# Feed-forward blocks that run over the batch boundary in a spectral mixing and ELU feed-forward kernel

## The chip, the cores and the metric

The kernel runs on one core of a Trainium2 chip. A core has TensorE (PE, matmuls into PSUM; its weight loads are listed apart as PEld), VectorE (DVE), ScalarE (ACT), GpSimd (POOL) and SyncE (SP, which issues most DMAs). The metric is device time in microseconds (us). The page and the trace come from one profiled execution.

## What is computed

The input x has 8 batches of 3008 tokens with 256 features. Each batch goes through a real Fourier transform along the tokens, a complex 256 x 256 product with bias, a soft threshold and the inverse transform. The result, taken as 24064 tokens, goes through a feed-forward layer of width 2048 with ELU.

```
X = np.fft.rfft(x, axis=1)
Yr = Xr @ w_r - Xi @ w_i + b_r
Yi = Xr @ w_i + Xi @ w_r + b_i
Yr = np.sign(Yr) * np.maximum(np.abs(Yr) - lam, 0.0)    # and Yi; lam = 0.01
y = np.fft.irfft(Yr + 1j * Yi, n=3008, axis=1)
h = y.reshape(24064, 256) @ w_in                        # 256 -> 2048
g = np.where(h > 0.0, h, np.exp(np.minimum(h, 0.0)) - 1.0)
out = g @ w_out                                         # 2048 -> 256
```

## The kernel before

**Feed-forward.** A batch is cut into blocks of TB = 512 tokens: five of 512 and one of 448. The hidden width is 16 tiles of 128, taken in pairs, so a block has NPAIR = 8 steps, a batch PER = 48, the program 384. Step i has two halves. `front(i)` (L675) runs four bf16 matmuls (L688), two hidden tiles by two halves of the 256 features, from yT (the transposed output of the inverse transform) into the PSUM tile hps, and then Exp on ScalarE (L701) into Et. `elu` (L719) clips Et, and one step later `finish_elu` (L706) makes gT with one VectorE operation. `back(i)` (L729) runs eight matmuls of 256 columns (L749, weights from gT, two hidden tiles by four groups of 128 tokens; in a block of 448 the last group has 64) that add into the PSUM tiles ps_o. It is issued LAG = 2 steps behind its front. After the eighth step of a block, ps_o is copied to osb (L763; L767 for the groups of a 448 block's end) and stored to DRAM by up to two DMAs for each group of 128 tokens (L774).

**Transforms.** The next batches' transforms are cut into units, of which a step takes at most one ahead of its front:

- A (L128): first stage of the transform, two matmuls from a loaded x tile, a cast by ScalarE; after each second unit a store DA (512 KB). Six units a batch, made two batches ahead of use.
- X (L165): reads Z, which `load_Z` loads back from DA; eight units of eight matmuls.
- M (L200): the complex product, four matmuls of 512 columns, twelve units; its threshold is done by VectorE and GpSimd.
- B (L227): first stage of the inverse, eight matmuls, six units; after each second unit a store DB (512 KB).
- Y (L268): reads Bs, which `load_Bs` (four DMAs of 384 KB, one for each fourth of the tokens) loads back from DB; eight matmuls of 94 columns and a cast into yT. Eight units, two for each fourth of the tokens: units 0 and 1 make tokens 0 to 751.

`plan(b)` (L783) writes the order by hand: `mid` is the list, `lead` the step at which it begins (1 in the first batch, else 0). Before, steps 0 to 3 carry Y2 to Y5, 4 to 11 the X units, 12 to 37 the M, B and A units with Y6 and Y7 among them, and the steps 38 to 44 and 46 are bare. Y0 and Y1 of the next batch stand at steps 45 and 47 (`yn`). The Bs loads follow A2 (step 34), the Z loads A5 (step 37).

**What depends on that.** The loop (L826) calls a step `free` if it has nothing planned. In a free step the clip is shared by GpSimd and VectorE (L724) and gT is made by L713; in a step with an M unit ScalarE does the whole clip (L698, L699); else VectorE clips alone (L726) and L715 makes gT. In calm free steps each third hps comes from the units' PSUM pool psF (one buffer), else from psH (two). Where a block ends in a step that is not free (`split`), the first copy of ps_o goes to VectorE. TensorE takes its instructions in the order written, and so does SP its DMA issues: stores of DA and DB, loads of Z and Bs, and outputs stand in one line and wait for each other's turn.

Of the kernel before, what the change touches and what calls it, by code (L numbers as in the profile page):

```python
# [9 lines left out]
AF = mybir.ActivationFunctionType  # L10
BF16 = mybir.dt.bfloat16
F32 = mybir.dt.float32
# [17 lines left out]
def kernel(  # L30
# [11 lines left out]
    nc = tc.nc  # L42
    P = nc.NUM_PARTITIONS

    B, S, D = x.shape
    assert D == 256 and S == N1 * N2
    DFF = moe_w_in.shape[1]
    E = moe_w_out.shape[1]
# [14 lines left out]
    w_in_s = constp.tile([P, 2, DFF], BF16, name="w_in_s")  # L63
# [24 lines left out]

    TB = 512
    NPAIR = NFT // 2  # L90
    NBLK = (S + TB - 1) // TB
    PER = NBLK * NPAIR
    LAG = 2
    n = B * PER
    WT = 2 * N1 * 8
# [10 lines left out]
    yT_of = {}  # L106
# [192 lines left out]
    with tc.tile_pool(name="stagep", bufs=1) as stagep:  # L299
# [90 lines left out]
        c1 = mix(dve, qcol, -2.0, pcol, ALU.mult, ALU.add)  # L390
        c0 = col(dve, c1, -1.0, ALU.mult, 1.0, ALU.add)
# [265 lines left out]
    for u in range(2):  # L657
# [9 lines left out]
    psO = ctx.enter_context(  # L667
        tc.tile_pool(name="psO", bufs=2, space=bass.MemoryType.PSUM, reuse_waits="tile")
    )
# [2 lines left out]
    g_of = {}  # L672
    po_of = {}

    def front(i, third, on_act):  # L675
        b, r = divmod(i, PER)
        blk, fp = divmod(r, NPAIR)
        bs = blk * TB
        nb = min(TB, S - bs)
        yT = yT_of[b]  # L680
        if third:
            hps = psF.tile([P, 2, TB], F32, name="hps", tag="fps")
        else:
            hps = psH.tile([P, 2, TB], F32, name="hps", tag="hps")
        for s in range(2):
            ft = 2 * fp + s
            for dt in range(2):
                nc.tensor.matmul(  # L688
                    hps[:, s, 0:nb], lhsT=w_in_s[:, dt, ft * P : ft * P + P],
                    rhs=yT[:, dt, bs : bs + nb], start=(dt == 0), stop=(dt == 1),  # L690
                )
        Et = late3.tile([P, 2, TB], F32, name="Et", tag="Et")
        E_ = Et[:, :, 0:nb]
        if i == n - 1:
            for s in range(2):
                nc.scalar.activation(E_[:, s], hps[:, s, 0:nb], AF.Exp)
        elif on_act:
            nc.scalar.activation(E_, hps[:, :, 0:nb], AF.Relu, scale=-1.0)  # L698
            nc.scalar.activation(E_, E_, AF.Exp, scale=-1.0)  # L699
        else:  # L700
            nc.scalar.activation(E_, hps[:, :, 0:nb], AF.Exp)  # L701
        return hps, Et, nb

    late_elu = []

    def finish_elu():  # L706
        for i, hps, Et, nb, whole in late_elu:
            E_, h_ = Et[:, :, 0:nb], hps[:, :, 0:nb]
            gT = late3.tile([P, 2, TB], F32R, name="gT", tag="gT")
            for s in range(2) if i == n - 1 else (slice(0, 2),):  # L710
                o, h, e = gT[:, s, 0:nb], h_[:, s], E_[:, s]
                if whole:
                    nc.vector.scalar_tensor_tensor(o, e, -1.0, h, ALU.add, ALU.max)  # L713
                else:
                    nc.vector.scalar_tensor_tensor(o, h, 0.0, e, ALU.max, ALU.add)  # L715
            g_of[i] = gT
        late_elu.clear()

    def elu(i, hps, Et, nb, on_pool, on_act):  # L719

        E_ = Et[:, :, 0:nb]
        if on_pool:
            for eng, s in ((nc.gpsimd, 1), (nc.vector, 0)):
                eng.tensor_scalar(E_[:, s], E_[:, s], 1.0, 0.0, ALU.min, ALU.max)  # L724
        elif not on_act:
            nc.vector.tensor_scalar(E_, E_, 1.0, -1.0, ALU.min, ALU.add)  # L726
        late_elu.append((i, hps, Et, nb, on_pool or on_act))

    def back(i, split):  # L729
        b, r = divmod(i, PER)  # L730
        blk, fp = divmod(r, NPAIR)
        bs = blk * TB
        nb = min(TB, S - bs)
        gT = g_of.pop(i)
        nsub = (nb + P - 1) // P
        if fp == 0:
            po_of[b, blk] = [
                psO.tile([P, 2, E], F32, name="ps_o", tag="outp") for _ in range((nsub + 1) // 2)
            ]
        po = po_of[b, blk]  # L740
        nq = (nsub + 1) // 2
        order = [(q, s) for q in range(nq) for s in range(2)]
        if i == n - 1:
            order = [(q, s) for s in range(2) for q in range(nq)]
        for q, s in order:
            ft = 2 * fp + s
            for i_ in range(2 * q, min(2 * q + 2, nsub)):
                t0, t1 = i_ * P, min(i_ * P + P, nb)
                nc.tensor.matmul(  # L749
                    po[q][0 : t1 - t0, i_ % 2, :], lhsT=gT[:, s, t0:t1],  # L750
                    rhs=w_out_r[:, ft, :], start=(ft == 0 and i_ % 2 == 0),
                    stop=(ft == NFT - 1), skip_group_check=True,
                )
        if fp < NPAIR - 1:
            return
        osb = late2.tile([P, 4, E], F32, name="osb", tag="osb")
        ov = out[b * S : b * S + S, :].rearrange("(r w j) e -> w r j e", w=4, j=8)
        last = i == n - 1
        for q in range(nq):
            k = min(2, nsub - 2 * q)  # L760
            copy = nc.vector.tensor_copy if (last and q) or (split and q == 0) else nc.scalar.copy
            if nb >= (2 * q + k) * P:
                copy(osb[:, 2 * q : 2 * q + k, :], po[q][:, 0:k, :])  # L763
            else:
                for e in range(k):
                    rows = min(P, nb - (2 * q + e) * P)
                    copy(osb[0:rows, 2 * q + e, :], po[q][0:rows, e, :])  # L767
            for i_ in range(2 * q, 2 * q + k):
                t, end = bs + i_ * P, min(bs + i_ * P + P, bs + nb)
                while t < end:  # L770
                    w, r0 = t // WT, t % WT // 8
                    t1 = min(end, (w + 1) * WT)
                    p0, n8 = t - bs - i_ * P, (t1 - t) // 8
                    (nc.scalar if last and i_ % 2 == 0 else nc.sync).dma_start(  # L774
                        ov[w, r0 : r0 + n8], osb[p0 : p0 + 8 * n8, i_, :]
                    )
                    t = t1
        del po_of[b, blk]

    def put(kind, b, *a):  # L780
        return ({"A": unit_A, "X": unit_X, "M": unit_M, "B": unit_B, "Y": unit_Y}[kind], (b, *a))

    def plan(b):  # L783

        f0 = [[] for _ in range(PER)]
        f1 = [[] for _ in range(PER)]
        n1, n2 = b + 1, b + 2
        mid = [("X", u) for u in range(8)] + [
# [4 lines left out]
        ]  # L793
        if n1 < B:
            lead, seq = int(b == 0), [("y", u) for u in range(2, 6)] + mid
            seq.insert(20, ("y", 6))
            seq.insert(24, ("y", 7))
            xs = (3, 8, 13)
            yn = (45, 47)
        else:  # L800
            lead, seq = 0, [("y", u) for u in range(2, 8)]
        for t, u in enumerate(seq, lead):
            if u[0] == "y":
                f0[t].append(put("Y", b, u[1]))
            elif u[0] == "A":
                if n2 < B:
                    f0[t].append(put("A", n2, u[1]))
            else:
                f0[t].append(put(u[0], n1, *u[1:]))
            if u == ("A", 2):  # L810
                f1[t] += [(load_Bs, (n1, w)) for w in range(4)]
            if u == ("A", 5) and n2 < B:
                f1[t] += [(load_Z, (n2, s0, s1)) for s0, s1 in ((0, 8), (8, NS))]
        if b == 0:
            f1[xs[0]].append((lambda: gate(Z_of[1][:, 16, 0:1]), ()))
        if n2 < B:
            for ci in range(3):
                f1[xs[ci]].append((load_x, (n2, ci)))
        if n1 < B:
            for u in range(2):  # L820
                f0[yn[u]].append(put("Y", n1, u))
        return f0, f1

    f0 = f1 = None
    bare = 0
    for i in range(n + LAG):  # L826
        if i < n:
            r = i % PER
            if r == 0:
                f0, f1 = plan(i // PER)  # L830
# [6 lines left out]
            on_act = any(f is unit_M for f, a in f0[r])  # L837
            h = front(i, calm and bare % 3 == 2, on_act)
# [42 lines left out]
```

## Time and profile before

| What | Value |
| --- | --- |
| time, median of 3 runs (lowest to highest) | 926.57 us (925.47 to 928.17) |
| profiled execution: its own time | 927.22 us |
| its span in the trace | 925.4 us |
| granted TensorE clock | 0.999 |
| busy: PE, DVE, ACT, POOL | 898.0, 754.0, 697.3, 268.3 us |
| back matmuls L749 | 3072 |
| front matmuls L688 (of 1536, as recorded) | 1463 |
| moved by DMA | 106.21 MB |

The median of the runs is what a change is measured by; the profiled execution is one run, of which everything about single instructions is known. A line of the profile's groups reads: source line, engine, operation, output <- inputs, partitions x elements, count | busy us, mean ns of one | idle time of the engine before them and what ended it. A line of the timeline reads: start in us, duration in us, engine, line, operation, count. Some matmul records are missing, weight loads are all there; so steps are timed here by the first weight load of their front (L688), of which each step has four.

### The profile page before, as it was taken

Reading aid. Unit: us, or ns where it says so; the run is one execution under the profiler, and the core shown is the slowest. Engines: PE = TensorE matmul, PEld = TensorE weight load, DVE = VectorE, ACT = ScalarE, POOL = GpSimd, SP = SyncE. Lnnn points to the kernel's source line nnn. Section 1 sums busy time; section 2 is a strip of 40 time slices with the busy share of each in tenths; the row PEclk is TensorE's granted clock in tenths of the full one; section 3 lists DMA queues with packets and bytes.
Section 4 is the critical chain, followed back from the end, with each engine's and each line's share of the span. In section 5 each row is a group of like instructions: output and inputs, shape, how many; then the busy total and the mean of one; then the engine's idle time right before and its main releaser. Section 6 shows DMA issues by size and latency. Waiting matters only on the chain.

```text
span 925.4 us, 16719 instructions
## 1 busy us (share of the span) xinstructions
PE 898.0 (97%) x6477; PEld 643.8 (70%) x6583; DVE 754.0 (81%) x898; ACT 697.3 (75%) x783; POOL 268.3 (29%) x352
## 2 busy tenths in 40 slices
PE   8879999999999999999999999999999999999997
PEld 3447667776677676776677766777777767677775
DVE  7868778887788777897788877887778877789997
ACT  6667787777868788687787778777786878676664
POOL 6801441133310441205402153113331044322332
PEclk9999999999999999999999999999999999999999
DMA  8984216621383224722166031752138002411011
GB/s 263 355 253 141 91 47 191 193 69 46 94 225 113 69 68 126 220 88 90 48 181 204 24 91 46 211 174 69 47 95 224 21 24 68 114 48 44 23 46 44
DMA packets 90655, 106.21 MB, mean 115 GB/s; under 512 B 5264, under 2 KB 81296, under 8 KB 87216
## 3 DMA queue, kind: packets, MB, share of 16 engines
q1 hardware_dynamic: 84320, 77.61, 30.0%
q0 software_dynamic: 5968, 27.26, 9.0%
q8 instruction: 51, 0.84, 0.4%
q10 hardware_dynamic: 288, 0.26, 0.1%
q14 instruction: 28, 0.23, 0.1%
HBM read 55.31 MB, written 49.81 MB: 114 GB/s over the span
## 4 chain that ended last, share of the span: by engine, by line
PE 72%; DVE 16%; ACT 3%; issue 3%; DMA 3%; POOL 1%; SPq 0%; DVEq 0%; ACTq 0%; POOLq 0%
PE ps_o L749 29%; PE hps L688 28%; PE mps L189 8%; DVE gT L713 7%; DVE Et L724 3%; PE bps L238 2%; DVE gT L715 2%; ACT Et L701 2%; PE yps L276 2%; PE aps L143 2%; DVE Et L726 2%; PE xps L174 1%; DMA Z<-DA 1%; DMA DA<-A 1%; DMA xt<-in_x_dram 1%
## 5 line engine op out<-in xcount | busy, mean ns | idle before, releaser
L749 PE MATMUL ps_o<-w_out_r,gT 128*128 128x256 f32 (+1 forms) x3072 | 486.4, 301 | 0.7 <-DVE gT L713 0.5
L749 PEld LDWEIGHTS ps_o<-w_out_r,gT 128*128 128x128 f32 (+1 forms) x3072 | 407.1, 186 | 61.2 <-DVE gT L713 14.4
L688 PE MATMUL hps<-yT,w_in_s 128*128 128x512 bf16 (+1 forms) x1463 | 383.5, 375 | 8.6 <-DVE gT L715 1.4
L701 ACT ACTIVATE Et<-hps 128x1024 f32<-128x1024 f32 (+1 forms) x299 | 300.7, 1006 | 85.7 <-PE hps L688 77.6
L713 DVE SCALAR_TENSOR_TENSOR gT<-Et,hps 128x1024 fp32r<-128x1024 f32 (+2 forms) x187 | 220.0, 1177 | 60.9 <-ACT Et L699 38.3
L715 DVE SCALAR_TENSOR_TENSOR gT<-hps,Et 128x1024 fp32r<-128x1024 f32 (+1 forms) x198 | 240.3, 1214 | 15.5
L688 PEld LDWEIGHTS <-w_in_s 128*128 128x128 bf16 x1536 | 131.5, 98 | 140.0 <-issue 21.7
L726 DVE TENSOR_SCALAR Et<-Et 128x1024 f32<-128x1024 f32 (+1 forms) x198 | 135.9, 686 | 45.5 <-ACT Et L701 40.1
L204 POOL TENSOR_SCALAR clip<-yb 128x512 f32<-128x512 f32 x84 | 51.6, 615 | 331.9 <-DVE yb L196 262.5
L724 POOL TENSOR_SCALAR Et<-Et 128x512 f32<-128x512 f32 (+1 forms) x102 | 64.8, 636 | 269.9 <-ACT Et L701 268.7
L698 ACT ACTIVATE Et<-hps 128x1024 f32<-128x1024 f32 x84 | 86.2, 1026 | 72.1 <-PE hps L688 71.0
L205 POOL TENSOR_TENSOR Y<-yb,clip 128x512 bf16<-128x512 f32 x84 | 107.3, 1277 | 7.0
L196 DVE TENSOR_TENSOR yb<-mps,bias_bc 128x512 f32<-128x512 f32 x96 | 65.8, 688 | 32.2 <-PE mps L189 23.6
L699 ACT ACTIVATE Et<-Et 128x1024 f32<-128x1024 f32 x84 | 88.8, 1057 | 2.7
L126 ACT CAST XT<-xps 128x768 bf16<-128x768 f32 x61 | 48.6, 799 | 16.6 <-PE xps L174 16.6
L126 ACT CAST yT<-yps 128x752 bf16<-128x752 f32 x63 | 49.5, 786 | 15.0 <-PE yps L276 15.0
L126 ACT CAST A<-aps 128x1024 bf16<-128x1024 f32 x45 | 45.3, 1010 | 15.7 <-PE aps L143 13.4
L189 PE MATMUL mps<-wcat_s,XT 128*128 128x512 bf16 x183 | 55.2, 379 | 1.1
L724 DVE TENSOR_SCALAR Et<-Et 128x512 f32<-128x512 f32 (+1 forms) x102 | 54.6, 536 | 0.3 <-ACT Et L701 0.2
L189 PE MATMUL mps<-wcat_r,XT 128*128 128x512 bf16 x171 | 53.5, 385 | 0.7 <-ACT XT L126 0.6
L189 PEld LDWEIGHTS <-XT 128*128 128x128 bf16 x384 | 30.3, 98 | 29.5 <-ACT XT L126 0.9
L251 ACT CAST Bz<-bps 128x1024 bf16<-128x1024 f32 x46 | 45.9, 999 | 3.2 <-PE bps L238 3.2
(104 smaller groups left out, 402.8 us busy)
## 6 DMA issues: line engine op xcount, KB each, us to landing
xt<-in_x_dram POOLq DMA_DIRECT2D x21, 1024.0 KB, 5.4
out_dram<-osb SPq DMA_DIRECT2D x158, 128.0 KB
Bs<-DB SPq DMA_DIRECT2D x32, 384.0 KB
DA<-A SPq DMA_DIRECT2D x21, 512.0 KB
DB<-Bz SPq DMA_DIRECT2D x21, 512.0 KB
Z<-DA SPq DMA_DIRECT2D x7, 1152.0 KB
Z<-DA SPq DMA_DIRECT2D x11, 384.0 KB
xt<-in_x_dram POOLq DMA_DIRECT2D x6, 512.0 KB, 6.3
```

The source lines that it names most:

```text
L126: nc.scalar.copy(dst, src)
L189: nc.tensor.matmul(ps, lhsT=XT[:, dt, c, o : o + P], rhs=wm[:, dt, :], start=(m == 0 and dt == 0), stop=(m == 1 and dt == 1),)
L205: nc.gpsimd.tensor_tensor(Y_of[b, q][:, i, :], yb[:], clip[:], ALU.subtract)
L688: nc.tensor.matmul(hps[:, s, 0:nb], lhsT=w_in_s[:, dt, ft * P : ft * P + P], rhs=yT[:, dt, bs : bs + nb], start=(dt == 0), stop=(dt == 1),)
L698: nc.scalar.activation(E_, hps[:, :, 0:nb], AF.Relu, scale=-1.0)
L699: nc.scalar.activation(E_, E_, AF.Exp, scale=-1.0)
L701: nc.scalar.activation(E_, hps[:, :, 0:nb], AF.Exp)
L713: nc.vector.scalar_tensor_tensor(o, e, -1.0, h, ALU.add, ALU.max)
L715: nc.vector.scalar_tensor_tensor(o, h, 0.0, e, ALU.max, ALU.add)
L724: eng.tensor_scalar(E_[:, s], E_[:, s], 1.0, 0.0, ALU.min, ALU.max)
L726: nc.vector.tensor_scalar(E_, E_, 1.0, -1.0, ALU.min, ALU.add)
L749: nc.tensor.matmul(po[q][0 : t1 - t0, i_ % 2, :], lhsT=gT[:, s, t0:t1], rhs=w_out_r[:, ft, :], start=(ft == 0 and i_ % 2 == 0), stop=(ft = ...
```

## The change

The feed-forward no longer sees batches: 24064 tokens are 47 blocks of 512, so the program has 376 steps, 47 for each batch's plan. A block may hold the end of one batch and the beginning of the next. In such a block (there are seven) each front matmul becomes two, one for each batch's yT, with 64 and 448, 128 and 384, 192 and 320, or 256 and 256 columns; a group of 128 tokens that holds both batches is stored by DMAs of its own for each. Every operation on hps, Et, gT and osb has full width.

Y0 and Y1 of the next batch stand at steps 38 and 39. A5 stands at step 37, in the first batch at step 40, behind them. The end of the order is B4, A0, B5, A1, Bs loads, A2 to A5; before it was A0, B4, A1, B5, A2, Bs loads, A3 to A5. B4 thus follows the last M unit, and the Bs loads are issued at step 33 (34 in the first batch, whose list begins a step later).

```diff
-    NBLK = (S + TB - 1) // TB
-    PER = NBLK * NPAIR
+    PER = S * NPAIR // TB
...
+    def pieces(t, k):
+        out_, c = [], 0
+        while c < k:
+            b, r = divmod(t + c, S)
+            e = min(k, c + S - r)
+            out_.append((b, r, c, e))
+            c = e
+        return out_
...
         for s in range(2):
             ft = 2 * fp + s
-            for dt in range(2):
-                nc.tensor.matmul(
-                    hps[:, s, 0:nb], lhsT=w_in_s[:, dt, ft * P : ft * P + P],
-                    rhs=yT[:, dt, bs : bs + nb], start=(dt == 0), stop=(dt == 1),
-                )
+            for b, t0, c0, c1 in pieces(blk * TB, TB):
+                for dt in range(2):
+                    nc.tensor.matmul(
+                        hps[:, s, c0:c1], lhsT=w_in_s[:, dt, ft * P : ft * P + P],
+                        rhs=yT_of[b][:, dt, t0 : t0 + c1 - c0],
+                        start=(dt == 0), stop=(dt == 1),
+                    )
...
-            for i_ in range(2 * q, min(2 * q + 2, nsub)):
-                t0, t1 = i_ * P, min(i_ * P + P, nb)
+            for i_ in range(2 * q, 2 * q + 2):
                 nc.tensor.matmul(
-                    po[q][0 : t1 - t0, i_ % 2, :], lhsT=gT[:, s, t0:t1],
+                    po[q][:, i_ % 2, :], lhsT=gT[:, s, i_ * P : i_ * P + P],
...
-            if nb >= (2 * q + k) * P:
-                copy(osb[:, 2 * q : 2 * q + k, :], po[q][:, 0:k, :])
-            else:
-                for e in range(k):
-                    rows = min(P, nb - (2 * q + e) * P)
-                    copy(osb[0:rows, 2 * q + e, :], po[q][0:rows, e, :])
+            copy(osb[:, 2 * q : 2 * q + 2, :], po[q][:])
...
-            ("M", 4, 1), ("B", 3), ("M", 5, 0), ("M", 5, 1), ("A", 0), ("B", 4), ("A", 1),
-            ("B", 5), ("A", 2), ("A", 3), ("A", 4), ("A", 5),
+            ("M", 4, 1), ("B", 3), ("M", 5, 0), ("M", 5, 1), ("B", 4),
+            ("A", 0), ("B", 5), ("A", 1), ("A", 2), ("A", 3), ("A", 4),
...
-            yn = (45, 47)
+            seq += [("A", 5), ("n", 0), ("n", 1)] if b else [("n", 0), ("n", 1), ("A", 5)]
...
+            elif u[0] == "n":
+                f0[t].append(put("Y", n1, u[1]))
...
-            if u == ("A", 2):
+            if u == ("A", 1):
                 f1[t] += [(load_Bs, (n1, w)) for w in range(4)]
```

More of the change, by code (lines that the diff above doesn't have):

```diff
@@ L90 @@
     NPAIR = NFT // 2
-    NBLK = (S + TB - 1) // TB
-    PER = NBLK * NPAIR
+    assert S * NPAIR % TB == 0 and S % (P // 2) == 0
+    PER = S * NPAIR // TB
     LAG = 2
@@ L673 @@
     po_of = {}
-    def front(i, third, on_act):
[L676 to L680, printed above, removed]
+    def pieces(t, k):
[6 more added lines that the diff above has]
+        return out_
+    def front(i, third, on_act):
+        blk, fp = divmod(i, NPAIR)
         if third:
@@ L686, in front @@
             ft = 2 * fp + s
-            for dt in range(2):
-                nc.tensor.matmul(
-                    hps[:, s, 0:nb], lhsT=w_in_s[:, dt, ft * P : ft * P + P],
-                    rhs=yT[:, dt, bs : bs + nb], start=(dt == 0), stop=(dt == 1),
-                )
+            for b, t0, c0, c1 in pieces(blk * TB, TB):
[5 more added lines that the diff above has]
+                    )
         Et = late3.tile([P, 2, TB], F32, name="Et", tag="Et")
-        E_ = Et[:, :, 0:nb]
+        E_ = Et[:]
         if i == n - 1:
             for s in range(2):
-                nc.scalar.activation(E_[:, s], hps[:, s, 0:nb], AF.Exp)
+                nc.scalar.activation(E_[:, s], hps[:, s], AF.Exp)
         elif on_act:
-            nc.scalar.activation(E_, hps[:, :, 0:nb], AF.Relu, scale=-1.0)
+            nc.scalar.activation(E_, hps[:], AF.Relu, scale=-1.0)
             nc.scalar.activation(E_, E_, AF.Exp, scale=-1.0)
         else:
-            nc.scalar.activation(E_, hps[:, :, 0:nb], AF.Exp)
-        return hps, Et, nb
+            nc.scalar.activation(E_, hps[:], AF.Exp)
+        return hps, Et
     late_elu = []
     def finish_elu():
-        for i, hps, Et, nb, whole in late_elu:
-            E_, h_ = Et[:, :, 0:nb], hps[:, :, 0:nb]
+        for i, hps, Et, whole in late_elu:
             gT = late3.tile([P, 2, TB], F32R, name="gT", tag="gT")
             for s in range(2) if i == n - 1 else (slice(0, 2),):
-                o, h, e = gT[:, s, 0:nb], h_[:, s], E_[:, s]
+                o, h, e = gT[:, s], hps[:, s], Et[:, s]
                 if whole:
@@ L717, in finish_elu, with elu @@
         late_elu.clear()
-    def elu(i, hps, Et, nb, on_pool, on_act):
-        E_ = Et[:, :, 0:nb]
+    def elu(i, hps, Et, on_pool, on_act):
+        E_ = Et[:]
         if on_pool:
@@ L726, in elu @@
             nc.vector.tensor_scalar(E_, E_, 1.0, -1.0, ALU.min, ALU.add)
-        late_elu.append((i, hps, Et, nb, on_pool or on_act))
+        late_elu.append((i, hps, Et, on_pool or on_act))
     def back(i, split):
-        b, r = divmod(i, PER)
-        blk, fp = divmod(r, NPAIR)
+        blk, fp = divmod(i, NPAIR)
         bs = blk * TB
-        nb = min(TB, S - bs)
         gT = g_of.pop(i)
-        nsub = (nb + P - 1) // P
+        nq = TB // P // 2
         if fp == 0:
-            po_of[b, blk] = [
-                psO.tile([P, 2, E], F32, name="ps_o", tag="outp") for _ in range((nsub + 1) // 2)
-            ]
-        po = po_of[b, blk]
-        nq = (nsub + 1) // 2
+            po_of[blk] = [
+                psO.tile([P, 2, E], F32, name="ps_o", tag="outp") for _ in range(nq)
+            ]
+        po = po_of[blk]
         order = [(q, s) for q in range(nq) for s in range(2)]
@@ L756, in back @@
         osb = late2.tile([P, 4, E], F32, name="osb", tag="osb")
-        ov = out[b * S : b * S + S, :].rearrange("(r w j) e -> w r j e", w=4, j=8)
         last = i == n - 1
         for q in range(nq):
-            k = min(2, nsub - 2 * q)
             copy = nc.vector.tensor_copy if (last and q) or (split and q == 0) else nc.scalar.copy
-            if nb >= (2 * q + k) * P:
-                copy(osb[:, 2 * q : 2 * q + k, :], po[q][:, 0:k, :])
-            else:
-                for e in range(k):
-                    rows = min(P, nb - (2 * q + e) * P)
-                    copy(osb[0:rows, 2 * q + e, :], po[q][0:rows, e, :])
[L768 to L778, printed above, removed]
+            copy(osb[:, 2 * q : 2 * q + 2, :], po[q][:])
+            for i_ in range(2 * q, 2 * q + 2):
+                for b, t, c0, c1 in pieces(bs + i_ * P, P):
+                    ov = out[b * S : b * S + S, :].rearrange("(r w j) e -> w r j e", w=4, j=8)
+                    while c0 < c1:
+                        w, r0 = t // WT, t % WT // 8
+                        k = min(c1 - c0, (w + 1) * WT - t)
+                        (nc.scalar if last and i_ % 2 == 0 else nc.sync).dma_start(
+                            ov[w, r0 : r0 + k // 8], osb[c0 : c0 + k, i_, :]
+                        )
+                        t, c0 = t + k, c0 + k
+        del po_of[blk]
     def put(kind, b, *a):
@@ L818, in plan @@
                 f1[xs[ci]].append((load_x, (n2, ci)))
-        if n1 < B:
-            for u in range(2):
-                f0[yn[u]].append(put("Y", n1, u))
         return f0, f1
```

## The prediction

> **What bounds the kernel now.** I read four views of the profile: the engines' busy time, the groups by shape, the timeline of TensorE's weight loads, and the DMA queue's timeline. The first gives the suspect.
>
> ```profile
> PE 898.0 (97%) x6477; PEld 643.8 (70%) x6583; DVE 754.0 (81%) x898; ACT 697.3 (75%) x783; POOL 268.3 (29%) x352
> ```
>
> TensorE (PE) is at 97%, but matmuls are pipelined, so this is only a hint. The groups by shape give the operations that the change touches.
>
> ```profile
> L749 PE MATMUL ps_o<-w_out_r,gT 128*128 128x256 f32 x2944 | 479.0, 302 | 0.7 <-DVE gT L713 0.5
> L688 PE MATMUL hps<-yT,w_in_s 128*128 128x512 bf16 x1207 | 324.2, 380 | 7.5 <-DVE gT L715 1.4 <-DVE yT L124 1.0 <-DVE gT L713 0.2
> L688 PEld LDWEIGHTS <-w_in_s 128*128 128x128 bf16 x1536 | 131.5, 98 | 140.0 <-issue 21.7 <-DVE gT L713 2.0 <-DVE yT L124 1.2
> L688 PE MATMUL hps<-yT,w_in_s 128*128 128x448 bf16 x256 | 59.3, 354 | 1.0 <-DVE gT L713 0.6
> L749 PE MATMUL ps_o<-w_out_r,gT 128*64 128x256 f32 x128 | 32.7, 278 | 0.0
> L276 PE MATMUL yps<-M,Bs 96*128 96x94 bf16 x512 | 32.4, 210 | 2.3 <-DMA Bs<-DB 1.8 <-ACT yT L126 0.6
> ```
>
> A mean (302, 380 ns) is latency; the price is the distance between starts, which the trace has for every instruction. Its medians: 216 ns for a front matmul of 512 columns, 189 for 448, 42 for the 94 columns of a Y unit, 113 to 118 for a back matmul, and as much (118) for one with a 64-wide weight. So 64 columns cost 216 - 189 = 27 ns, or 0.42 ns each, and 216 - 512 x 0.417 = 2.5 ns come on top; a back matmul does not get cheaper with fewer tokens. Steps that carry no unit should then take 4 x 216 + 8 x 117 = 1.80 us with 512 tokens and 4 x 189 + 8 x 117 = 1.69 us with 448. The timeline of weight loads in the last batch shows just that (start, duration):
>
> ```profile
> 866.63 0.55 PEld L688 LDWEIGHTS <-w_in_s 128*128 128x128 bf16 x4
> ...
> 868.47 0.55 PEld L688 LDWEIGHTS <-w_in_s 128*128 128x128 bf16 x4
> ...
> 870.35 0.55 PEld L688 LDWEIGHTS <-w_in_s 128*128 128x128 bf16 x4
> ```
> ```profile
> 910.66 0.49 PEld L688 LDWEIGHTS <-w_in_s 128*128 128x128 bf16 x4
> ...
> 912.36 0.49 PEld L688 LDWEIGHTS <-w_in_s 128*128 128x128 bf16 x4
> ...
> 914.05 0.49 PEld L688 LDWEIGHTS <-w_in_s 128*128 128x128 bf16 x4
> ```
>
> 448-token steps are 1.70 and 1.69 us apart. 512-token steps are 1.84 and 1.88 here, 1.80 at best, and 1.85 on average over twelve (881.42 to 903.57). Steps with a unit follow the same sum: Y and X steps 2.16 (1.80 + 8 x 43 ns), M steps 2.66 (1.80 + 4 x 216 ns), A steps 2.26. TensorE's own work sets the end almost everywhere; VectorE is close behind in bare steps (its rows of 1217 and 562 ns make 1.78 us).
>
> **The change part by part.** *Steps.* The program has 376 steps of 512 tokens where it had 320 of 512 and 64 of 448. Front columns are the same; 64 back matmuls go (3072 to 3008). On paper: 64 x 1.69 - 56 x 1.80 = 7.4 us, all on the bound. What goes with them on other engines (8 Exps of ScalarE, 8 pairs of VectorE operations, 15 narrow copies of L767) lies beside TensorE; I count it as nothing.
>
> *The end of a batch, where stalls count too.* I time a step from its first front weight load to the next step's. Before, the stretch from step 37 to the next batch's step 0 is 11 steps and takes 20.8 to 20.9 us in five of seven batches (698.88 to 719.74, say), 21.1 in one, 21.7 in the first. The sum of TensorE's work there is 3 x 1.80 + 8 x 1.69 + 3 Y units x 0.36 = 20.0, so 0.9 us is stall: 0.23 at step 38 (2.03), where bare steps begin and the ELU changes its form, 0.24 after the block's end at step 41 (1.93), and 0.32 at step 45 (2.01), which carries a Y unit between bare steps; the rest is small. After, it is 10 steps: 10 x 1.80 + 3 x 0.36 = 19.1, and I allow 0.6 of stall: one change to bare steps instead of two (0.25), a block's end (0.2), and 0.15 for the 1.85 against 1.80. That makes 19.7, a gain of 1.2 us in each of 7 batches: 8.4. The last batch has eight steps of 1.70 less and seven of 1.85 more: 0.7. The last step's Exps and ELU are 512 wide: -0.1.
>
> *The crossing blocks.* Seven blocks hold two batches; in each of their 8 steps four front matmuls become eight, 224 more pairs of weight load and matmul. Split widths are 64, 128, 192 and 256 beside the rest of 512, with 64 pairs each of 64, 128 and 192. From below: 224 x 2.5 ns = 0.6 us, if pace stays linear. From above: every piece shorter than its weight load costs the row's 98 ns, not 29, 56 or 83: 64 x (69 + 42 + 15) ns = 8.1, with the 0.6 makes 8.7 us. The nearest row is the Y unit: 94 columns with a weight load each, 98 to 100 ns long, yet 42 ns apart, so loads do hide behind each other. Only the 64-column pieces are narrower; at 42 ns they add 64 x 13 = 0.8. I take 1.0.
>
> The Trainium skill (TensorE: Matmul & The Clock Gate, Back-to-back issue gap) says that a stream of load and matmul pairs sustains about 81 ns a pair at 128 columns; by it the pieces of 64 and 128 would cost 64 x (52 + 25) ns = 4.9 us more, 5.5 in all. The trace's 42 ns at 94 columns speaks against it here.
>
> *The first two Y units at steps 38 and 39.* They issue the same 16 matmuls and 2 casts; two steps that were not bare (45, 47) become bare and two others not: no sum changes. A crossing front waits for the cast of the unit at 39, 0.79 us of ScalarE, with all later fronts and backs queued behind it on TensorE; at the closest, in the first batch, the A5 unit, a front and a back (over 2 us) lie between. The new risk is Bs: it is asked for 5 steps ahead, not 11. The queue before:
>
> ```profile
> 471.14 0.36 SPq L259 DMA_DIRECT2D DB<-Bz  x1
> 472.31 2.52 SPq L774 DMA_DIRECT2D out_dram<-osb  x4
> 475.00 1.87 SPq L265 DMA_DIRECT2D Bs<-DB  x4
> 476.97 3.69 SPq L156 DMA_DIRECT2D DA<-A  x2
> ```
>
> The store of B5 lands at 474.4 (3.2 us), the first Bs load at 479.3, the fourth at 483.6. Y0 needs the first only: 8.2 us after the store's issue, with 512 KB of output queued between; now 512 KB of the store of A1 lies there instead. Y0 comes six steps after B5, 2.23 + 5 x 2.26 = 13.5 us, less 1.7 from B5's matmuls to its store: 11.8 us. Slack 3.6 us; 1.3 in the first batch, whose list begins a step later, and 6 x 1.85 - 1.7 - 8.2 = 1.2 in the seventh, without A units. Cost nothing; at the other end, if the first load landed with the fourth (12.5), 0.7 us a batch, 4.9 in all.
>
> *The order B4, A0, B5, A1.* B4 now follows an M step, where A0 did. Before, A after M takes 2.46 (0.2 over), and B after M 2.63 against 2.43 elsewhere: the same 0.2 on another unit. Nothing, give or take 0.2 a batch (1.4). SP's queue keeps the same stores, with the Bs loads a step earlier and ahead of some output stores. In the first batch A5 and the Z loads come at step 40: from A5's matmuls to the last Z landing took 16.5 us (478.47 to 494.95); X0 follows 11 steps later, 6 x 1.85 + 5 x 2.16 = 21.9 us. Nothing.
>
> **Sum.** 8.4 + 0.7 - 0.1 - 1.0 = 8.0 us off the profiled execution's 927.22 (span 925.4): 919.2. It lay 0.65 above the median of 926.57, so the median should be **918.6**.
>
> **Rivals.** *Stalls stay or move.* A bare step of 512 has TensorE at 1.80 and VectorE at 1.78, so any lateness is paid by both; block ends now fall at another step in each batch, in X and A steps too, where a step costs 0.17 more at the fourth step of each batch (2.33 against 2.16). Two such stalls more and a second change of form a batch are 0.6 x 7 = 4.2: 922.8. Against it: VectorE has 0.25 us to spare in X and Y steps. Chance 0.12.
>
> *Narrow pieces have a floor.* If a weight load (98 ns) hides only behind a matmul as long as itself, no pair is shorter than 98 ns, which gives 918.6 + 7.7 = 926.3; half of that, 922.5. For it, the length of the row; against it, 42 ns at 94 columns. Chance 0.07. By the Trainium skill's pace for such pairs (the section named above) it would be 918.6 + 4.5 = 923.1.
>
> *Bs comes late (slower).* TensorE takes its work in order: if the load of step 38 is not there, fronts and backs wait behind it, seven times. Up to 3.6 us of delay (1.2 in two batches) costs nothing. To end 2.8 us above now, it must stall 10.8 / 7 = 1.5 us a batch, so the first load must land 13.3 us after B5's store, later than even the fourth did (12.5). At 2 us of stall: 918.6 + 14 = 932.6. For it: SP stands in order behind the store of A1 and the waits of the queue. Chance 0.05.
>
> *All stalls go.* If the 10 steps take 19.1 and the crossing 0.6, the gain is 12.7: 914. Chance 0.08.
>
> **How the numbers follow.** The forecast, 915.5 to 922, has 0.68. The range 914.0 to 923.5 adds most of the rival of stalls (0.11), a half floor (0.02) and half of the best case (0.04), 0.85 in all; the strict floor, a late Bs and a still better end are left out. Within 0.3% (2.8 us, about what this measurement can tell from no change: its three runs span 2.7) fall the floor (0.06), the worst of the stalls (0.01) and a small lateness of Bs (0.02): 0.09. Slower: the rest of a late Bs (0.03) and a floor that costs still more (0.01). Faster: 0.68 + 0.11 + 0.08 = 0.87.
>
> **What would show it.** Right: 3008 back matmuls; bare steps at 1.80 to 1.85 us throughout, no 1.69; the end of a batch 10 steps in 19.5 to 19.9 us; 64-column fronts some 30 to 42 ns apart; no wait of Y's weight loads for Bs beyond the start. Wrong: 64-column pieces 80 to 100 ns apart; a wait of TensorE for Bs at step 38; bare steps above 1.95 us; a stall in X or A steps where a block ends.

## Result, and the profile after

| | before | after |
| --- | --- | --- |
| time, median of 6 runs each (lowest to highest) | 927.72 us (925.47 to 929.57) | 922.75 us (922.12 to 923.39) |
| span of the profiled execution | 925.4 us | 920.3 us |
| granted TensorE clock | 0.999 | 0.997 |

The ratio is 0.9947, 95% interval 0.9932 to 0.9962: 5.0 us faster, where 8.0 were forecast. With three more runs, the kernel before came out 1.15 us above the 926.57 that the forecast started from; its median of 918.6 is thus missed by 4.2 us, and its gain by 3.0. A second measurement of the unchanged after kernel, beside the experiments, gave 922.06 us and 0.9950 (0.9937 to 0.9964). The busy line and the groups of after:

```profile
PE 897.0 (97%) x6711; PEld 648.5 (70%) x6711; DVE 753.4 (82%) x880; ACT 695.0 (76%) x767; POOL 263.3 (29%) x344
...
L752 PE MATMUL ps_o<-w_out_r,gT 128*128 128x256 f32 x3008 | 473.0, 300 | 0.9 <-DVE gT L720 0.9
...
L695 PE MATMUL hps<-yT,w_in_s 128*128 128x512 bf16 (+7 forms) x1728 | 388.5, 352 | 6.7 <-DVE gT L720 2.5
```

The 3008 back matmuls are there (L752, was L749), and the fronts (L695, was L688) have 1504 + 224 = 1728 matmuls. The shares hardly moved; what changed has to be read step by step. As in the prediction, a step is timed from its front's first weight load to the next step's. By batches and stretches (us, sums over the batches named):

| stretch | before | after | saved | forecast |
| --- | --- | --- | --- | --- |
| step 37 to the batch's end, batches 1 to 7 | 147.1 | 140.3 | 6.8 | 8.4 |
| steps 28 to 36, batches 1 to 7 | 149.1 | 148.7 | 0.4 | 0 |
| steps 0 to 27, batch 1 | 68.3 | 67.3 | 1.0 | 0 |
| steps 0 to 27, batches 2 to 7 | 404.4 | 408.0 | -3.6 | 0 |
| batch 8 | 88.0 | 87.3 | 0.7 | 0.6 |
| crossing blocks | | | in the rows above | -1.0 |
| first front to last front | 856.9 | 851.6 | 5.3 | 8.0 |

The end of a batch did what was forecast: 19.54 to 20.01 us in batches 2 to 7 (forecast 19.7), where the kernel before took 20.79 to 21.07. Two things went wrong. The first batch kept 21.83, and the steps behind the batch's start, of which the forecast said nothing, got longer by 0.3 to 1.1 us in each later batch. Single steps that stand out (us, in brackets the same kind of step without a stall):

| where | after | number |
| --- | --- | --- |
| step 0 of batches 2 to 8 | 2.46, 2.61, 2.60, 2.65, 2.54, 2.62, 2.57 (2.16 in before) | +0.42 on average, 2.9 in all |
| the B step behind an M step in which a block ends: batch 2 step 27, batch 7 step 16, batch 5 step 30 | 2.84, 2.84, 2.77 (2.48, 2.48, 2.29) | +0.36 to 0.48 |
| the same with a Y unit next: batch 2 step 19, batch 6 step 23 | 2.47, 2.49 (2.13) | +0.35 |
| batch 2 step 21, two steps behind the late step 19 | 3.00 (2.66) | +0.34 |
| batch 1, steps 37 and 45 | 3.12, 2.61 (2.11, 1.87) | +1.0, +0.74 |
| batch 7, step 38 | 2.57 (2.15) | +0.42 |
| given back: step 11 of batches 2 to 7 | 2.50 (2.72 in before, where a block always ended two steps earlier) | -0.23 each, -1.4 in all |

Step 0 is the largest. The timeline of after around step 0 of the fourth batch (start, duration, then engine, line, operation, count; in brackets the idle time before it and what ended it):

```profile
386.52 1.22 DVE L720 SCALAR_TENSOR_TENSOR gT<-Et,hps 128x1024 fp32r<-128x1024 f32 x1
...
387.33 0.10 PEld L695 LDWEIGHTS <-w_in_s 128*128 128x128 bf16 x1
...
387.80 1.03 PE L695 MATMUL hps<-yT,w_in_s 128*128 128x320 bf16 x8 [0.26 <-DVE gT L720]
387.80 0.80 PEld L695 LDWEIGHTS <-w_in_s 128*128 128x128 bf16 x7 [0.37 <-issue]
```

The first weight load is ready at 387.33, but the matmuls start at 387.80, when VectorE has finished gT (386.52 + 1.22 = 387.74). That gT is of step 45, two steps back. Fronts outside the free steps have two buffers for hps (psH), so a front writes where the front two steps before it wrote, once gT has read that. Within the bare steps each third front takes the buffer psF instead, and TensorE gets further ahead of VectorE than two buffers allow. The loop gives psF to a front only while the next two steps are bare too, so step 44 is the last to get it. The two fronts behind it still find a buffer last used three steps before; the third one, step 0 of the next batch, is the first that needs the buffer of two steps before, and waits until the lead is gone.

In the first batch, Y0 waits for Bs (rows of the timeline of after):

```profile
149.56 0.69 DVE L733 TENSOR_SCALAR Et<-Et 128x1024 f32<-128x1024 f32 x1 [0.28 <-ACT Et L709]
150.16 0.36 PEld L276 LDWEIGHTS <-Bs 96*128 96x128 bf16 x8 [1.05 <-DMA Bs<-DB]
```

And a block's end in an M step (step 29), with a B step behind it (step 30, fifth batch):

```profile
569.08 1.06 ACT L707 ACTIVATE Et<-Et 128x1024 f32<-128x1024 f32 x1
...
570.05 0.57 ACT L763 COPY osb<-ps_o 128x512 f32<-128x512 f32 x1
...
570.51 1.02 ACT L251 CAST Bz<-bps 128x1024 bf16<-128x1024 f32 x1
...
571.58 0.30 PEld L143 LDWEIGHTS aps<-xt,M 128*128 128x128 f32 x2 [0.38 <-ACT Bz L251]
```

In an M step ScalarE does two passes over Et. The copy of ps_o (0.57 us) stands in its line ahead of the cast Bz, which then ends at 571.53, and TensorE's next unit (A0) waits 0.38 us for it, since both units use the same PSUM buffer. In before the block ends stood at the same steps in each batch, none of them in an M step with a B step next; now they move on by one step a batch. In after ten blocks end in an M step: the five with a B step next are late, the five with another M step next are not (2.63 to 2.68 us for the step behind them, as without a block's end).

### The profile page after: what moved, and what is told of

It is laid out like the page before. It is cut to its first block, busy times and chain, and to the rows that moved or that the text cites. A ratio compares the mean times of both kernels' runs of the same rounds, so it can differ in the third digit from the quotient of the medians.

```text
span 920.3 us, 17019 instructions
## 1 busy us (share of the span) xinstructions
PE 897.0 (97%) x6711; PEld 648.5 (70%) x6711; DVE 753.4 (82%) x880; ACT 695.0 (76%) x767; POOL 263.3 (29%) x344
## 4 chain that ended last, share of the span: by engine, by line
PE 63%; DVE 21%; issue 5%; ACT 5%; DMA 4%; POOL 1%; DVEq 0%; SPq 0%; ACTq 0%; POOLq 0%
PE hps L695 24%; PE ps_o L752 23%; DVE gT L720 11%; PE mps L189 9%; DVE Et L731 4%; ACT Et L709 2%; PE bps L238 2%; DVE gT L722 2%; DVE Et L733 2%; PE xps L174 2%; PE aps L143 2%; PE yps L276 2%; DMA Z<-DA 1%; DMA DA<-A 1%; POOL Et L731 1%
## 5 line engine op out<-in xcount | busy, mean ns | idle before, releaser
L752 PE MATMUL ps_o<-w_out_r,gT 128*128 128x256 f32 x3008 | 473.0, 300 | 0.9 <-DVE gT L720 0.9
L752 PEld LDWEIGHTS ps_o<-w_out_r,gT 128*128 128x128 f32 x3008 | 399.2, 189 | 55.5 <-DVE gT L720 13.2
L695 PE MATMUL hps<-yT,w_in_s 128*128 128x512 bf16 (+7 forms) x1728 | 388.5, 352 | 6.7 <-DVE gT L720 2.5
L709 ACT ACTIVATE Et<-hps 128x1024 f32<-128x1024 f32 x291 | 299.8, 1030 | 84.5 <-PE hps L695 78.0
L720 DVE SCALAR_TENSOR_TENSOR gT<-Et,hps 128x1024 fp32r<-128x1024 f32 (+1 forms) x179 | 216.8, 1212 | 52.8 <-ACT Et L707 36.6
L722 DVE SCALAR_TENSOR_TENSOR gT<-hps,Et 128x1024 fp32r<-128x1024 f32 x198 | 242.0, 1222 | 16.3 <-DVE Et L733 0.5
L695 PEld LDWEIGHTS <-w_in_s 128*128 128x128 bf16 x1728 | 144.2, 98 | 137.3 <-issue 26.9
L733 DVE TENSOR_SCALAR Et<-Et 128x1024 f32<-128x1024 f32 x198 | 136.9, 691 | 45.3 <-ACT Et L709 37.9
L706 ACT ACTIVATE Et<-hps 128x1024 f32<-128x1024 f32 x84 | 86.3, 1027 | 72.9 <-PE hps L695 72.4
L731 POOL TENSOR_SCALAR Et<-Et 128x512 f32<-128x512 f32 x94 | 59.8, 637 | 279.3 <-ACT Et L709 278.0
L731 DVE TENSOR_SCALAR Et<-Et 128x512 f32<-128x512 f32 x94 | 54.1, 576 | 0.9 <-ACT Et L709 0.8
```

The lines of the kernel that those rows point to most:

```text
L695: nc.tensor.matmul(hps[:, s, c0:c1], lhsT=w_in_s[:, dt, ft * P : ft * P + P], rhs=yT_of[b][:, dt, t0 : t0 + c1 - c0], start=(dt == 0), sto ...
L706: nc.scalar.activation(E_, hps[:], AF.Relu, scale=-1.0)
L709: nc.scalar.activation(E_, hps[:], AF.Exp)
L752: nc.tensor.matmul(po[q][:, i_ % 2, :], lhsT=gT[:, s, i_ * P : i_ * P + P], rhs=w_out_r[:, ft, :], start=(ft == 0 and i_ % 2 == 0), stop=( ...
```

## Experiments

Seven kernels besides the unchanged one. All are edits of after but E2, which is the kernel before with another plan. E3, E8 and E9 have one run each, and the steps of every kernel come from one profile. Start-up and the first batch differ between profiles of one kernel (the first front at 58.5 and the first batch 110.7 us long in one profile of after, 112.0 long in the other), so gains of under 1 us are read from the later steps, not from the time.

**E1: are the crossing pieces dear?** Fronts of crossing blocks stay whole; they read only the batch with the larger part, so the other batch's tokens are left out of them.

```diff
-            for b, t0, c0, c1 in pieces(blk * TB, TB):
+            b, t0, c0, c1 = max(pieces(blk * TB, TB), key=lambda p: p[3] - p[2])
+            t0, c0, c1 = min(t0, S - TB), 0, TB
+            if 1:
```

> Leaves out part of the computation: in the seven crossing blocks each front matmul takes all 512 columns from one batch (the one with more tokens in the block), so the other batch's tokens there are not used; the 224 extra pairs of weight load and matmul go, all else stays. Forecast's step (narrow pieces pace like their columns, 1.0 us for all): 0.6 to 1.4 us faster than the changed kernel, and the step at a batch's start that carries Y3 still takes about 2.6 us (2.16 is TensorE's sum). Rival (the pieces have a floor, or the eight loads of a crossing front are what makes that step 0.45 us long): 3 us faster or more, and that step falls to 2.16 to 2.2.

Measured: 923.26 us, ratio to before 0.9954 (0.9938 to 0.9969), which is not told apart from after; this profile's first front starts 1.8 us later (60.3). By steps, the 56 crossing steps are 0.9 us shorter in all and first front to last front 0.8 us (850.8). Step 0 keeps 2.48 to 2.65. So the pieces cost 0.8 to 0.9 us, as forecast (1.0), and neither they nor a floor under them is the missing part. The weight loads of the bare steps 41 to 43 of after's first batch, whose fronts are cut into 448 and 64 columns, show it too:

```profile
156.80 0.95 PEld L695 LDWEIGHTS <-w_in_s 128*128 128x128 bf16 x8
...
158.73 0.93 PEld L695 LDWEIGHTS <-w_in_s 128*128 128x128 bf16 x8
...
160.61 0.93 PEld L695 LDWEIGHTS <-w_in_s 128*128 128x128 bf16 x8
```

Eight loads where there were four, and the steps are 1.93 and 1.88 us apart.

**E2: the plan alone.** Before's blocks (five of 512 and one of 448 in each batch, 384 steps) with after's order and its Y0 and Y1 at steps 38 and 39. The cut shows the count of steps, against after.

```diff
-    PER = S * NPAIR // TB
+    NBLK = (S + TB - 1) // TB
+    PER = NBLK * NPAIR
...
-        blk, fp = divmod(i, NPAIR)
+        b, r = divmod(i, PER)
+        blk, fp = divmod(r, NPAIR)
```

> The kernel before with its 48 steps and 448-token blocks, and only the plan changed: first two Y units at steps 38 and 39, order B4, A0, B5, A1, Bs loads, A2 to A5. Theory (a front waits for the gT of two steps before, since hps has two buffers outside psF; VectorE is behind after bare steps of 512 tokens but not after bare steps of 448): steps 28 to 37 about 0.15 us a batch shorter, the stall of 0.32 at step 45 gone, no stall of 0.45 at the second step of the next batch, first batch about 1 us longer at step 37 to 38 for Bs: in all 1.5 to 3 us faster than the kernel before. Rival (any change from bare steps to Y steps costs 0.45, whatever the width): the batch's second step takes 2.5 or more here too, and the time is that of the kernel before within 1 us.

Measured: 927.55 us, ratio 1.0004 (0.9994 to 1.0013): no gain. Gains and losses cancel. Step 45, where before has 2.01 us, falls to 1.71, and steps 28 to 36 of batches 2 to 6 are 0.12 to 0.16 us shorter. But the last step of batches 2 to 7 takes 2.62 to 2.66 where 1.69 + 0.36 = 2.05 is TensorE's work, and step 37 of the first batch 3.27, for Bs, as in after. The last step in the timeline of E2 (second batch):

```profile
278.34 1.09 DVE L713 SCALAR_TENSOR_TENSOR gT<-Et,hps 128x896 fp32r<-128x896 f32 x1
...
279.49 0.92 PE L688 MATMUL hps<-yT,w_in_s 128*128 128x448 bf16 x4 [0.47 <-DVE gT L713]
```

My theory, that the late step needs the 512-token bare steps with their small margin on VectorE, fell: it comes behind bare steps of 448 as well. It belongs to the way out of the bare steps with psF, of 448 and of 512 alike: in E2 the last front with psF is step 44, and the late one is again the third behind it, step 47, which is itself a bare step. In before it was step 42, and the late one step 45. The plan moved the stall of step 45 to the batch's end. On before's blocks the plan gains nothing, so the gain of the change is put down to the blocks; the new blocks with the old plan were not run.

**E3: Bs two steps earlier.** The four Bs loads are issued with B5, ahead of A1's store.

```diff
-            if u == ("A", 1):
+            if u == ("B", 5):
```

> The changed kernel with the Bs loads issued in the step of B5, ahead of the store of A1 and, in the first batch, of the four output stores. Theory (in the first batch Y0 waits 1.05 us for the first Bs load, which had 512 KB of output and 512 KB of A1's store ahead of it in SP's queue): step 37 of the first batch falls from 3.12 to about 2.15 us, the rest stays, about 1 us less in the span. Rival (the load is late since B5's own store is late): no change of that step.

Measured: 968.0 us, 45 us slower than after, 43 of them between step 28 and the end of a batch. A gain of 1 us had been my theory; it fell. The timeline of E3 in step 36 of the second batch:

```profile
272.54 1.01 ACT L126 CAST A<-aps 128x1024 bf16<-128x1024 f32 x1 [5.74 <-DMA DA<-A]
...
273.60 0.50 PEld L143 LDWEIGHTS aps<-xt,M 128*128 128x128 f32 x2 [4.98 <-ACT A L126]
```

The A tile has two buffers. A1's store now stands on SP behind four Bs loads that wait for B5's store; ScalarE sits idle for 5.74 us ahead of the cast of a later A unit, until a store has freed the tile, and TensorE 4.98 us, until that cast is done. In the second to sixth batches step 36 takes 7.3 to 9.3 us and step 37 3.2 to 4.0, and in the first batch step 37 takes 9.3. With two A buffers the change therefore needs this store ahead of the Bs loads.

**E4: the block-end copies.** Where a block ends in an M step, both copies of ps_o go to VectorE.

```diff
-            copy = nc.vector.tensor_copy if (last and q) or (split and q == 0) else nc.scalar.copy
+            copy = nc.vector.tensor_copy if (last and q) or (split and q < split) else nc.scalar.copy
...
-                back(i - LAG, True)
+                back(i - LAG, 2 if on_act else 1)
```

> The changed kernel; where a block ends in a step with an M unit, both copies of ps_o go to VectorE instead of one to ScalarE. Theory (block ends now walk over the plan, and where one falls in the M step ahead of a B step, ScalarE with Relu, Exp, copy and the cast of B is over 2.5 us late and psF and hps come free late): the stalls of 0.34 to 0.5 us after steps 18 and 26 of the second batch, 29 of the fifth, 22 of the sixth and 15 of the seventh go, 1.5 to 2.5 us less. Rival (VectorE is the late one there): these steps get longer by 0.3 to 0.6 us each and other M steps with a block's end too, 2 us slower or more.

Measured: 920.39 us, ratio 0.9928 (0.9912 to 0.9945). Steps 0 to 27 of the second batch fall from 68.54 to 67.40 us, of the sixth from 67.97 to 67.53, of the seventh from 68.20 to 67.74, and steps 28 to 36 of the fifth from 21.96 to 21.42: 2.6 us, just the batches in which a block ended in an M step ahead of a B step. By time alone E4 is not told apart from after (0.9947, 0.9932 to 0.9962); the steps tell them apart. The same place as in after's fifth batch:

```profile
568.92 1.28 DVE L763 COPY osb<-ps_o 128x512 f32<-128x512 f32 x2
...
569.99 0.99 ACT L251 CAST Bz<-bps 128x1024 bf16<-128x1024 f32 x1
```

Both copies are VectorE's, the cast Bz starts 0.66 us behind the first weight load of its step where it started 1.13 behind, and TensorE no longer waits for it. That the walking block ends cost some 2.3 to 2.6 us is shown: 0.3 of it is open, since step 21 of the second batch took 2.68 us in the profiles of E3 and E8 too, which changed nothing there.

**E8: step 0 and VectorE.** The clip of step 45 is left out in each batch, so VectorE has some 0.6 us less to do there.

```diff
-        if on_pool:
+        if on_pool and i % PER == PER - 2:
+            pass
+        elif on_pool:
```

> Leaves out part of the computation: the clip of Exp in step 45 of each batch (both halves, VectorE and GpSimd); all other work stays. Theory (the first front of a batch that comes behind a Y unit waits for the gT of step 45, because hps has two buffers once psF goes back to the units, and VectorE makes gT late): gT of step 45 is ready about 0.6 us earlier, and the step that took 2.4 to 2.65 us (from the front with Y2 ahead of it to the front with Y3 ahead of it) falls to about 2.2 in seven batches, 2.5 to 3 us in all. Rival (that step waits for psF, for ScalarE's cast or for the crossing weight loads): no change there.

Measured: 919.38 us. Step 0 takes 2.25, 2.22, 2.20, 2.17, 2.15, 2.17, 2.15 us in batches 2 to 8, from 2.46 to 2.65: 2.7 us less in all. Some of it comes back later: step 2 takes 2.39 and 2.43 in batches 7 and 8, from 2.17 and 2.23. The timeline at the fourth batch:

```profile
384.51 2.35 DVE L720 SCALAR_TENSOR_TENSOR gT<-Et,hps 128x1024 fp32r<-128x1024 f32 x2
...
387.14 0.85 PEld L695 LDWEIGHTS <-w_in_s 128*128 128x128 bf16 x8
387.18 1.04 PE L695 MATMUL hps<-yT,w_in_s 128*128 128x320 bf16 x8
```

gT of steps 44 and 45 follow each other and end at 386.86, before the front asks for the buffer at 387.14, and its eight matmuls run without a gap. So step 0 waits for VectorE's gT of step 45.

**E9: or is it psF itself?** Step 44 of the first seven batches takes its hps from psH and not from psF. This does not take the lead away: step 41 still has psF and is then the last front that has it (in the first batch nothing changes, since its last is step 42).

```diff
-            h = front(i, calm and bare % 3 == 2, on_act)
+            h = front(i, calm and bare % 3 == 2 and (r != 44 or i >= 7 * PER), on_act)
```

> The changed kernel; step 44 of the first seven batches takes its hps from the two buffers of psH instead of psF. Theory (the third buffer lets TensorE run ahead, and the lead is given back when bare steps end): the stall at the end gets smaller, but steps 43 to 46 get longer by as much, and the stretch from step 39 to the next batch's step 2 stays at 20.0 to 20.4 us or grows by up to 0.3. Rival (the use of psF at step 44 is the cause of the stall): the stretch falls by 0.4 us a batch, some 2.5 us in all.

Measured: 928.7 us, 6 us slower than after. Step 0 does fall (2.22 and 2.17 us in the third and fourth batch, from 2.61 and 2.60), but in the second to fourth batch step 44 rises from 1.87 to 2.15 us to 2.59 to 2.90, and step 46 from 2.13 to 2.18 us to 2.76 to 2.81. The stretch grows by 0.9 us a batch, where the theory allowed 0.3. Step 44 of the third batch in the timeline of E9:

```profile
382.04 1.22 DVE L720 SCALAR_TENSOR_TENSOR gT<-Et,hps 128x1024 fp32r<-128x1024 f32 x1
...
383.31 1.03 PE L695 MATMUL hps<-yT,w_in_s 128*128 128x320 bf16 x8 [0.60 <-DVE gT L720]
```

The stall has moved, and its rule shows. In before, E2, after and E9 the front that is late is the third behind the last one with psF, and it waits for the gT of two steps before:

| kernel and batches | last front with psF | late step | it takes (without the stall) |
| --- | --- | --- | --- |
| before, 2 to 7 | 42 | 45 | 1.94 to 2.05 (1.69) |
| E2, 2 to 7 | 44 | 47 | 2.62 to 2.66 (2.05) |
| after, 2 to 7 | 44 | 0 of the next batch | 2.54 to 2.65 (2.16) |
| after, 1 | 42 | 45 | 2.61 (1.87) |
| after, 7, whose bare steps begin at 34 | 35 | 38 | 2.57 (2.15) |
| E9, 2 to 7 | 41 | 44 | 2.55 to 2.90 (1.80 to 2.15) |

E9's second late step, 46, is the fifth behind the last front with psF. After's first batch has the same pair: step 45 (+0.74) is the third behind step 42, and the fifth is the second batch's step 0 (+0.30). Where Y steps follow the late front, as in batches 3 to 8 of after, no second one is seen (2.14 to 2.23 us two steps later). So at step 44 the third buffer is no cost: it saves some 1.4 us in steps 44 to 46 of a batch and gives back 0.42 at step 0. Why an exit within the bare steps is late by more, and twice, is not settled; VectorE's 1.78 us in a bare step of 1.80, against its 0.25 us to spare in a Y step, would fit, but no run tried it.

**E10: copies and the first batch's outputs.** E4, and the four output stores that SP issues ahead of the Bs loads in the first batch are issued behind them.

```diff
+                        if i == 31:
+                            held_out.append(args)
+                        else:
+                            out_q.dma_start(*args)
...
+            if i == 34:
+                for a in held_out:
+                    nc.sync.dma_start(*a)
```

> The changed kernel with both copies of ps_o on VectorE where a block ends in an M step, and with the four output stores of the block that ends at step 33 of the first batch issued behind the Bs loads. Theory (Y0 of the first batch waits 1.05 us since those 512 KB and the 512 KB of A1's store lie ahead of Bs in SP's queue): step 37 of the first batch falls from 3.1 to about 2.15 us, and the time is 3.4 us under the changed kernel, about 919.4 where that takes 922.8. Rival (B5's store itself is late, or the stores slow the loads wherever they stand): that step keeps 0.5 us or more of its stall, and the gain is 2.4 us.

SP's queue in the first batch, after and then E10:

```profile
139.45 0.36 SPq L259 DMA_DIRECT2D DB<-Bz  x1
140.77 2.54 SPq L770 DMA_DIRECT2D out_dram<-osb  x4
143.41 0.54 SPq L156 DMA_DIRECT2D DA<-A  x1
144.12 2.71 SPq L265 DMA_DIRECT2D Bs<-DB  x4
```
```profile
139.27 0.36 SPq L259 DMA_DIRECT2D DB<-Bz  x1
141.67 0.37 SPq L156 DMA_DIRECT2D DA<-A  x1
143.21 1.76 SPq L265 DMA_DIRECT2D Bs<-DB  x4
145.07 2.60 SPq L844 DMA_DIRECT2D out_dram<-osb  x4
```

Measured: step 37 of the first batch falls from 3.12 to 2.11 us, so the wait for Bs was the output stores' doing: A1's store still stands ahead of the loads. In all 919.45 us, ratio to before 0.9926 (0.9914 to 0.9939), 2.6 us under the after kernel measured beside it (922.06); 3.4 were hoped for, and the rest is within what the first batch and the start differ by. It beats before, and all its five runs lie below the five of after, though it is not told apart from E4 by time.

## Why the prediction was right in kind and wrong in size

The 922.75 us lie inside the stated range (914.0 to 923.5) but above the narrower forecast of 915.5 to 922: the direction and the main terms held, and three allowances were too small.

**Held.** Steps of 512 tokens instead of 448, on a path set by TensorE: bare steps mostly take 1.80 to 1.93 us, the end of a batch 10 steps and 19.5 to 20.0 us. The crossing: 0.8 to 0.9 us for 1.0, and the linear rule goes on below the 94 columns that were the nearest row. Front matmuls of the crossing blocks start 29 ns apart at 64 columns, 56 at 128, 82 at 192, 109 at 256, 216 at 512, with a 98 ns weight load for each. The rival with a floor falls. The Trainium skill (TensorE: Matmul & The Clock Gate, Back-to-back issue gap) gives about 81 ns a pair at 128 columns; the 56 ns measured here decide against it, and by the forecast's estimate from its pace the crossing would have cost 5.5 us. The order B4, A0, B5, A1 was put at nothing and gave 0.15 us a batch.

**Failed, one: the allowance for stalls, "one change to bare steps instead of two (0.25)".** It removed before's stall at step 45 from the sum and looked for no successor. E2, E8 and E9 show what that stall was: TensorE leaving the steps with psF with a lead of a third hps buffer, which two buffers can't hold. A plan with one bare stretch has one such exit, now at step 0 of the next batch, just past the stretch that I summed: step 0 is 0.42 us too long on average, seven times, 2.9 us. The forecast's own list had the stall of step 45 (0.32); its cause was misread, as an effect of a Y unit between bare steps.

**Failed, two: "a block's end (0.2)" counted once a batch.** The rival in which stalls stay or move had the mechanism (a block's end falls at another step in each batch), but I gave it 0.12. That its 922.8 us is what was measured is luck: it stood for a gain of 3.8 us, where 5.0 were measured against a kernel before that came out 1.15 slower, and its 4.2 us were to come in equal parts from seven batches, with stalls at block ends in X and A steps among them. What spoke against it in the forecast was VectorE's spare time in X and Y steps. E4 shows that the engine was ScalarE and the place M steps ahead of B steps, in four of the batches only: 2.6 us, partly paid back by step 11, two steps behind a place where a block no longer ends (1.4). In X and Y steps a block's end costs 0.2 us two steps later, once a batch, as it did before.

**Failed, three: Bs in the first batch, slack 1.3 us.** I counted A1's store in place of the output ahead of the Bs loads. In the first batch both lie there, 512 KB each, and Y0 waited 1.05 us: the sign of being wrong that I had named, a wait for Bs at step 38, came there. E10 takes that away. In the other batches Bs cost nothing, as forecast. At step 45 of the first batch, whose last front with psF is step 42, a front waits for gT as at step 0 elsewhere (0.74); no run tried that one by itself.

**The sum.** The three and step 45 come to 2.9 + 2.6 + 1.0 + 0.7 = 7.2 us. Step 11 (1.4), the order (0.15 in six batches, 0.9) and a shorter wait for Z at step 4 of the first batch (1.0, not seen in every profile) give 3.3 back. Net 3.9, where the traces miss 8.0 - 5.3 = 2.7; the rest of 1.2 is the last batch (0.5 better than forecast without its step 0) and the batch ends (some 0.8 better, the crossing counted), spread over steps too small to be named. These sums rest on one profile of each kernel; in the second profile of after, first front to last front took 853.0 us and not 851.6, since the first batch waited longer for Z.

## What to carry to other kernels

Sum a change over the stretch that it touches and some steps beyond it, as many as there are buffers: an engine that leaves a stretch ahead of its consumer pays where the buffers become fewer, and that is outside. When a period changes (48 steps to 47 with blocks of 8), list where each periodic event now falls in every period, and what stands beside it on each engine. Before a load is issued earlier on an in-order queue, list every store that it passes and the buffer that the store frees.

## What the runs showed that I had not expected

A weight load of 98 ns did not bound matmuls of 64 columns: pairs of load and matmul, each with its own 128x128 bf16 weights, ran 29 ns apart, on the same line as 216 ns at 512 columns. And one store moved behind four loads in SP's queue (E3) cost 45 us, nine times what the whole change gained.
